# Memory attention and a maxout FFN on one core: who issues the first loads, how many transfers k and the last outputs take

## The chip, the cores and the metric

The kernel runs on one core of a Trainium2 chip. Its engines are TensorE (PE; PEld is its weight load), VectorE (DVE), ScalarE (ACT), GpSimd (POOL) and SyncE (SP); SP, ScalarE and GpSimd issue DMA transfers, which 16 DMA engines carry out. The metric is the time of one execution on the device in microseconds, the median of several runs.

## The reference

Eight batches of eight heads, 576 positions, 64 values a head and 32 memory slots; then a feed-forward layer over the 4608 rows of 512. All inputs and the output are float32.

```python
# q, k, v: (8, 8, 576, 64); phi: (8, 8, 576, 32); w1, w2, w3: (512, 768); w_out: (768, 512)
a = softmax(phi, axis=2)                        # over the 576 positions
k_m = einsum('bhsm,bhsd->bhmd', a, k)
v_m = einsum('bhsm,bhsd->bhmd', a, v)
attn = softmax(q @ k_m.T / 8, axis=-1)          # over the 32 slots
x = (attn @ v_m) as rows of (batch, position), columns of (head, value)
h = maximum(maximum(x @ w1, x @ w2), x @ w3)
out = h @ w_out
```

## The kernel before

The program has no loop over batches at run time. All steps are Python functions, and a long string of tokens, written out by hand, gives the order in which they emit their instructions: `B0@1` is part 0 of step `B` for batch 1, and a `!` swaps the engine that does the step's side work. Each engine runs its own instructions in that order and waits on semaphores for the others. Two strings of this kind matter here: the tokens (lines 782 to 809) and the PSUM banks (lines 143 to 151), which are handed out in order of request.

**Loads.** Tokens `L`, `H` and `J` load phi, k, v and q of a batch, `Y` the weights. k, v, q and the weights are cast to bfloat16 on the way and are issued by GpSimd (lines 97, 112, 119, 126), as is phi for all batches but the first (line 93). For batch 0, `load_ph` has SP issue two transfers, one for each half of the head pairs (line 91), and k comes as two transfers too: tokens `H2@0`, then `H0@0`, both through `load_kv` (line 97). The first instruction of ScalarE is the load of its table of functions (line 62). Each transfer of GpSimd takes the next of eight semaphores and waits until the transfer eight before it has landed; SP and ScalarE share another eight, taken in turn in the order of the program. SP, ScalarE's sends and the last outputs all count there. At the end (traced as the last line of the launch code, L837) SP waits for the last transfer on each of these semaphores in their order.

**Attention of a batch.** `E` is exp of phi (ScalarE, line 234), `B` multiplies it with k, v and a column of ones (TensorE, line 256), `N` and `K` norm and transpose the result, `Q` transposes q, `S` makes the scores and their exp (lines 342, 351). For batch 0 TensorE runs products of a zero tile (`Z`, line 164) while it waits.

**The feed-forward layer.** `D` folds v_m into the weights (line 453). w3 is subtracted from w1 and w2, so that the maximum can be taken in fewer steps; `V` does these subtractions in pieces (`w_diff`, line 218) and is emitted for pieces 0, 2 and 1. `F` multiplies the weights with the attention (line 504) and takes the maximum (line 517). The product with w_out is done by `T` (`ffn2`, lines 667 to 685) for batches 0 and 1 and for the rows between two batches, and by `P` (`products`, line 615) for the others: seven products that VectorE and ScalarE combine into four quarters of an output tile `ot`. `products` has SP send a tile of 512 KB when its second half is done (line 652); for the last batch each half is sent alone, 256 KB.

**The end.** `T4@7` calls `ffn2_last`: the last 128 rows are made in two halves of 256 columns. VectorE copies the left half from PSUM and SP sends it (lines 737, 738); ScalarE copies and sends the right half (lines 740, 741). The tile that both write is the buffer of an output tile of batch 6, since `opool` has four buffers.

Of the kernel before, what the change touches and what calls it, by code (L numbers as in the profile page):

```python
# [15 lines left out]
def kernel(  # L16
# [12 lines left out]
    nc = tc.nc  # L29
# [29 lines left out]

    nc.scalar.preload_act_table_set("natural_log_exp_and_others")
    KV, KS = NP * NC * D, D + 1
    K1 = NP * NC * KS
    ones_k = [const.tile([P, D + KV], BF16, name=f"ko{i}") for i in range(2)]
# [19 lines left out]
    def load_ph(b):  # L85
        ph = inp.tile([P, NP, NC, M], FP32, name="ph", tag="ph")
        loaded.setdefault(b, {})["ph"] = ph
        dst = ph.rearrange("p j c m -> p j (c m)")
        if b == 0:
            for h in halves:  # L90
                nc.sync.dma_start(out=dst[:, h], in_=by_pair(phi, b)[:, h])
        else:
            nc.gpsimd.dma_start(out=dst, in_=by_pair(phi, b))

# [31 lines left out]
        nc.gpsimd.dma_start(out=wo_sb, in_=moe_w_out.rearrange("(t p) c -> p t c", p=P))  # L126

    load_ph(0)

    warm = const.tile([P, BANK], BF16, name="warm")  # L130
    nc.vector.memset(warm, 0.0)  # L131
# [21 lines left out]
    def one_bank():  # L153
        return psum[:, int(next(banks))]
# [57 lines left out]

    def w_diff(n, swap):

        c, end = n * BANK, (n + 1) * BANK
        while c < end:
            e = min(end, (c // DF + 1) * DF)
            (nc.gpsimd if swap else nc.vector).tensor_tensor(  # L218
                out=w12[:, :, c:e],
                in0=w12[:, :, c:e],  # L220
                in1=w_sb[:, :, 2, c % DF : c % DF + e - c],
                op=ALU.subtract,
            )
            c = e
# [356 lines left out]
    def products(b, i, swap):  # L581

        s, a = sums(b), blocks(b)
        wp3 = wp3s[b]

        def plain(r, c):
            return lambda k, q: a[r][c][:, k, q]

        def summed(n):
            src = a[1][0] if n == 2 else s[min(n, 2)]  # L590
            return lambda k, q: src[:, k, q]

        def w_plain(i, j):
            c = slice(CH * j, CH * (j + 1))
            return lambda k: wo_sb[:, KT * i + k, c] if k < KT else wp3[:, i, c]

        def w_summed(n):
            return lambda k: tw[:, n, k] if k < KT else twb[b % 2][:, n]

        lhs, rhs, name = [  # L600
            (summed(0), w_summed(0), "y"),
            (plain(0, 0), w_plain(0, 0), "x"),
            (plain(0, 1), w_plain(1, 0), "z"),
            (summed(3), w_plain(1, 1), "y"),
            (summed(1), w_summed(1), "x"),
            (summed(2), w_summed(2), "x"),
            (plain(1, 1), w_summed(3), "x"),
        ][i]
        acc = quads.setdefault(b, {})
        if i < 3:  # L610
            acc[name] = one_bank()
        po = acc[name]
        for k in range(KT + 1):
            for q in range(2):
                nc.tensor.matmul(  # L615
                    po[:, q * CH : (q + 1) * CH],
                    lhsT=lhs(k, q),
                    rhs=rhs(k),
                    start=(i < 3 and k == 0 and q == 0),
                    stop=(k == KT and q == 1),  # L620
                    skip_group_check=True,
                )
        x = po.rearrange("p (q n) -> p q n", q=2)

        def copy(out_, in_):
            if swap:
                nc.vector.tensor_copy(out=out_, in_=in_)
            else:
                nc.scalar.copy(out=out_, in_=in_)  # L629

        if i in SNAP:
            t = ln if i == 0 else work.tile([P, S], FP32, name="snap", tag="r")
            t = acc[SNAP[i]] = t[:, 0:DM].rearrange("p (q n) -> p q n", q=2)
            copy(t, x)
        acc[i] = True
        done = [2] if i == 2 else [i] if i > 4 else [4] if 3 in acc and 4 in acc else []
        for n in done:
            if ("ot", n // 5) not in acc:
                acc["ot", n // 5] = opool.tile([P, 2, DM], FP32, name="ot")
            ot = acc["ot", n // 5][:, :, slice(0, CH) if n in (2, 6) else slice(CH, DM)]  # L640
            if n == 6:
                copy(ot, x)
            else:
                if n == 4:
                    x = acc["y"].rearrange("p (q n) -> p q n", q=2)
                y = acc[{2: "m1", 4: "u2", 5: "m5"}[n]]
                nc.vector.tensor_tensor(out=ot, in0=x, in1=y, op=ADD)
            if n in (4, 6) or b == B - 1:
                r0 = b * S + (b % 2) * HP
                rows = out[r0 : r0 + 2 * TW].rearrange("(q r p) c -> p q r c", q=2, r=2)  # L650
                c = slice(0, DM) if b < B - 1 else slice(0, CH) if n in (2, 6) else slice(CH, DM)
                nc.sync.dma_start(
                    out=rows[:, :, n // 5, c], in_=acc["ot", n // 5][:, :, c]
                )

    osts = {}

    def ffn2(b, t, swap):

# [2 lines left out]
        c0 = S - HP if t == 4 else (b % 2) * (S + HP) + t * P  # L662
        if b == B - 1:
            return ffn2_last(b, c0)
        po = one_bank()
        for n, fc in enumerate(fts[b]):
            nc.tensor.matmul(  # L667
                po,
                lhsT=hT[:, row(fc), c0 : c0 + P],
                rhs=wo_sb[:, fc, :],  # L670
                start=(n == 0),
                stop=False,
            )
        for g in range(NG):
# [31 lines left out]
    def ffn2_last(b, c0):  # L706
# [18 lines left out]
        for i, (c, po) in enumerate(zip(cs, pos)):  # L725
# [9 lines left out]
            rows = out[r0 : r0 + P, c]  # L735
            if i == 0:
                nc.vector.tensor_copy(out=ot[:, c], in_=po)
                nc.sync.dma_start(out=rows, in_=ot[:, c])
            else:
                nc.scalar.copy(out=ot[:, c], in_=po)  # L740
                nc.scalar.dma_start(out=rows, in_=ot[:, c])

    def issue(b, n, swap):
# [29 lines left out]
            "W": lambda: w3_t(i, swap),  # L773
            "g": lambda: send(i),
            "d": lambda: fold_begin(i),
            "O": lambda: w3_o(i, swap),
            "V": lambda: w_diff(i, swap),
            "Z": lambda: warm_up(i),
# [1 line left out]


    for w in """
        E@0 H2@0 H0@0 L3@0 Z25@0 B0@0 Y2@0 I@0 N0@0 Z2@0 K0@0! Q0@0 Q1@0 Z9@0 S@0 Z2@0
        M0@0 M1@0 R0@0 R1@0 W0@0 Y3@0 W1@0 W2@0 Z6@0 O1@0 H3@0 O3@0 O2@0 H1@0 X1@0 B1@0
        X0@0 N1@0 K1@0 O0@0 Y0@0 D1@0! D0@0! D3@0 F8@0 Y1@0 F10@0! L0@1 L1@1 F6@0 J0@1
        F0@0! F2@0! D2@0 D4@0 F4@0 F1@0 F3@0 F5@0 F11@0 F7@0 V0@0! E@1 F9@0 B0@1 N0@1
        T2@0! J1@1 Q0@1 L2@1 Q1@1 V2@0 K0@1! T1@0 S@1 B1@1 V1@0 L3@2 N1@1 M1@1 a0@1 s0@1
        R1@1 c0@1 K1@1 T3@0 D2@1 m0@1! D0@1 X1@1 L1@2 X0@1 D1@1 Q0@2 L0@2 T0@0! L2@2
        L1@3 Q1@2 L0@3 r0@2 F8@1! F4@1 F6@1! F7@1 E@2 F10@1! F2@1 F5@1 F0@1 g2@0 B@2
        D3@1 L2@3 L3@3 N@2 F9@1 F3@1 K@2! F11@1 g1@0 S@2 F1@1 D1@2! E@3 L1@4 U2@9 D0@2  # L790
        D3@2 T3@1 U0@9 T4@1! L0@4 r0@3 a@2 s@2 c@2 D2@2 B@3 L2@4 m@2! U2@2 X@2 F10@2 N@3
        F2@2 F11@2 F4@2 F0@2 K@3! L3@4 Q0@3 Q1@3 F6@2 F1@2 F8@2 g0@0 F3@2 S@3 F7@2 a@3
        F5@2 g3@0 s@3 F9@2 r0@4! E@4 U0@2 c@3 L0@5 U1@9 m@3! T2@1 X@3 U3@9 D0@3 D3@3
        T0@1! T1@1 L1@5 D2@3 B@4 D1@3! N@4 P1@2! L2@5 Q1@4 U1@2 F2@3 F6@3 F3@3 F8@3 L3@5
        U3@2 L1@6 U0@3 A0@2! Q0@4 K@4! F4@3! F0@3 F9@3 P2@2! A1@2! S@4 A2@2! A3@2! F5@3
        E@5 a@4 P4@2 F1@3 r0@5 P0@2 L2@6 F10@3 L0@6 s@4 F7@3 c@4 P5@2 m@4 D1@4! D3@4
        U1@3 F11@3 P3@2 A0@3! D2@4 B@5 A2@3! N@5 D0@4 X@4 T4@3! L1@7 A1@3! F10@4 Q0@5
        K@5 F0@4 L3@6 Q1@5 P6@2! S@5 r0@6! F11@4 F2@4! F1@4 L0@7 F6@4 F4@4! P1@3 F8@4
        a@5 s@5 U2@3 D2@5 D3@5 c@5 P2@3! E@6 m@5 A3@3! F5@4 P4@3 F3@4 F9@4 P0@3 D1@5!
        X@5 B@6 N@6 L2@7 D0@5 P5@3 U3@3 F8@5! F7@4 P3@3! r0@7! L3@7 U0@4 F2@5! F10@5 E@7  # L800
        U0@5 F3@5 Q0@6 A0@4! U1@4 P6@3 F11@5 F4@5 Q1@6 F6@5 F9@5 K@6! F0@5 A2@4! U2@4
        F5@5 S@6 F7@5 A1@4! a@6 A3@4! B@7 N@7 s@6 D3@6 D1@6! P0@4 P1@4 U3@4 K@7! P2@4!
        F1@5 Q1@7 P4@4 c@6 D0@7 D1@7 D0@6 P3@4 P5@4 U0@6 Q0@7 m@6 X@6 D2@6 D3@7 D2@7!
        A0@5! T4@5 S@7 A1@5! P6@4 F0@6 a@7 s@7 F4@6 F10@6 F1@6 c@7 F2@6 U2@5 F6@6 P1@5
        F3@6 F7@6 U1@5 P2@5 F8@6 A3@5! F9@6 F11@6 P4@5 m@7 X@7 F5@6 P0@5! F6@7 F10@7!
        A2@5! F2@7 P3@5! F4@7! F0@7 P5@5 F8@7! F1@7 F11@7 A0@6! U3@5 P6@5 F5@7 F9@7 U0@7
        A1@6 U1@7 A2@6 F3@7 U1@6 P1@6 F7@7 P0@6 P2@6! P4@6 U2@6 P1@7 A0@7 A3@6 U3@6 A1@7
        U3@7! P2@7! P5@6! P3@6 U2@7! A2@7 A3@7 P4@7 P6@6 P0@7! P5@7 P3@7! P6@7 T4@7!
    """.split():
        n, b = w.rstrip("!").split("@")  # L810
        issue(int(b), n, w.endswith("!"))
# [30 lines left out]
```

## Time and profile before

| | us |
|---|---|
| median of three runs | 162.17 (161.5, 162.17, 162.24) |
| profiled execution | 162.39 |
| its span | 160.6 (1.77 us of the execution lie outside it) |
| TensorE busy | 149.8 |
| VectorE, ScalarE, GpSimd busy | 118.5, 98.2, 104.3 |
| GpSimd's queue, SP's queue, ScalarE's queue: share of the 16 DMA engines' span | 70.9%, 15.3%, 2.2% |
| HBM read, written | 39.32 MB, 9.44 MB |

The granted TensorE clock is full throughout (1.0). In the page, the span is cut into 40 slices of 4 us; a digit is the busy share in tenths. In a timeline a line holds the start, the duration, the engine, the line of the kernel, the operation and, in brackets, the idle time ahead of it with what ended it. A "q" behind an engine's name (SPq) marks its issuing of transfers. In the windows a row holds the stretch and its length, the busy time of PE, PEld, DVE, ACT and POOL, the granted clock, the DMA engines' share and GB/s. The packet and landing records are the trace's lists of the DMA engines' packets and of the 16 completions of each transfer, one an engine.

### The profile page before, as it was taken

The page shows a single profiled execution, that of the slowest core. Times are in us where ns is not written, and L with a number is a line of the kernel's source. Part 1 is how long each engine was busy: PE and PEld are TensorE (multiplying, and loading weights), DVE is VectorE, ACT ScalarE, POOL GpSimd, SP SyncE. Part 2 cuts the span into 40 slices and gives each one's busy share as a digit, 9 for nine tenths or more (in the row PEclk, how much of TensorE's full clock was granted, in tenths as well). Part 3 has the DMA queues.
Part 4 walks back from the last instruction along what each step waited for, and adds up shares of the span by engine and source line. Part 5 has one row for each costly group of instructions (what it writes and reads, how often), then busy time and mean ns, then how long its engine had stood idle before and what let it go on. Part 6 is the DMA issues. An engine that isn't in the chain of part 4 may idle for free.

```text
span 160.6 us, 5165 instructions
## 1 busy us (share of the span) xinstructions
PE 149.8 (93%) x2219; PEld 100.4 (62%) x2228; DVE 118.5 (74%) x205; ACT 98.2 (61%) x140; POOL 104.3 (65%) x98
## 2 busy tenths in 40 slices
PE   7978698979897999999999999999999999999991
PEld 2433444654455537636877577787774888888871
DVE  2023803699897897897998789898989869799851
ACT  3205435742786699997777789888876944224210
POOL 7932101993039949968999996999969996910000
PEclk9999999999999999999999999999999999999999
DMA  5999999999999999999999999999803500330374
GB/s 150 164 201 203 201 209 214 279 207 212 209 276 245 276 233 261 285 262 282 268 231 209 259 260 254 261 173 170 271 0 134 196 6 0 131 131 4 150 279 159
DMA packets 22342, 31.78 MB, mean 198 GB/s; under 512 B 1072, under 2 KB 17456, under 8 KB 22320
## 3 DMA queue, kind: packets, MB, share of 16 engines
q0 software_dynamic: 16096, 21.43, 70.9%
q1 hardware_dynamic: 5504, 8.85, 15.3%
q10 hardware_dynamic: 720, 1.18, 2.2%
q8 instruction: 17, 0.28, 0.7%
q14 instruction: 5, 0.04, 0.1%
HBM read 39.32 MB, written 9.44 MB: 304 GB/s over the span
## 4 chain that ended last, share of the span: by engine, by line
PE 63%; DMA 25%; POOL 6%; issue 2%; ACT 1%; DVE 1%; POOLq 0%
PE psum L504 23%; PE psum L615 23%; DMA w_sb<-in_moe_w_dram 14%; DMA kvr<-in_v_dram 10%; PE psum L667 6%; PE psum L453 4%; PE psum L256 3%; PE psum L342 2%; POOL qq L112 1%; DMA out_dram<-ot 1%; POOL kvr L97 1%; POOL ko L97 1%; PE psum L676 1%; PE psum L685 1%; POOL w_sb L119 1%
## 5 line engine op out<-in xcount | busy, mean ns | idle before, releaser
L504 PE MATMUL psum<-hx,wp 128*128 128x288 bf16 x384 | 53.2, 286 | 0.1
L504 PEld LDWEIGHTS <-wp 128*128 128x128 bf16 x384 | 36.3, 98 | 11.6 <-issue 2.1
L517 DVE TENSOR_TENSOR hx<-psum,h 128x576 bf16<-128x576 f32 x48 | 34.8, 749 | 6.3 <-PE psum L504 4.5
L177 ACT CAST wp<-psum 128x1024 bf16<-128x1024 f32 (+1 forms) x29 | 27.5, 993 | 4.6 <-PE psum L453 4.4
L175 ACT ACTIVATE h<-psum 128x576 bf16<-128x576 f32 x34 | 21.5, 655 | 7.2 <-PE psum L504 6.6
L615 PEld LDWEIGHTS <-hx 128*128 128x128 bf16 x192 | 18.4, 98 | 3.5 <-issue 1.1
L667 PE MATMUL psum<-wo_sb,hx 128*128 128x512 bf16 x60 | 15.6, 380 | 0.3
L351 ACT ACTIVATE e<-psum 128x576 bf16<-128x576 f32 x16 | 9.5, 649 | 6.2 <-PE psum L342 6.2
L164 PE MATMUL psum<-warm 128*128 128x512 bf16 x42 | 12.0, 440 | 1.4 <-DVE warm L131 1.2
L615 PEld LDWEIGHTS <-w_sb 128*128 128x128 bf16 x120 | 11.6, 98 | 2.4 <-issue 0.8
L321 DVE STREAM_TRANSPOSE qT<-qq 128x576 f32<-128x576 f32 x16 | 11.9, 760 | 1.1 <-DMA qq<-in_q_dram 1.0
L107 POOL COPY kvr<-ko 128x2304 bf16<-128x2304 bf16 x3 | 6.3, 2111 | 8.8 <-DMA ko<-in_k_dram 8.8
L629 ACT COPY snap<-psum 128x512 f32<-128x512 f32 x11 | 6.5, 594 | 8.7 <-PE psum L615 8.7
L540 POOL TENSOR_TENSOR w_sb<-hx 128x1024 bf16<-128x1024 bf16 x5 | 10.6, 2121 | 1.6 <-DVE hx L517 1.6
L234 ACT ACTIVATE e<-ph 128x1152 bf16<-128x1152 f32 (+1 forms) x9 | 9.6, 1067 | 2.4 <-DMA ph<-in_phi_dram 2.4
L218 POOL TENSOR_TENSOR w_sb<-w_sb 128x2048 bf16<-128x2048 bf16 x1 | 4.1, 4052 | 10.6 <-PE psum L453 10.6
L179 DVE TENSOR_SCALAR h<-psum 128x576 bf16<-128x576 f32 x14 | 10.3, 746 | 0.7 <-PE psum L504 0.6
L667 PEld LDWEIGHTS <-hx 128*128 128x128 bf16 x66 | 5.9, 98 | 7.5 <-issue 1.7
L256 PEld LDWEIGHTS <-e 64*32 64x32 bf16 x720 | 7.3, 89 | 5.1 <-issue 3.6
L427 POOL TENSOR_TENSOR t<-t,sm 128x1152 bf16<-128x1152 bf16 x4 | 8.5, 2124 | 3.0 <-DVE sm L420 1.7
L540 POOL TENSOR_TENSOR twb<-wp 128x256 bf16<-128x256 bf16 x11 | 7.4, 675 | 4.2 <-ACT wp L177 4.2
L177 ACT COPY ot<-psum 128x512 f32<-128x512 f32 x9 | 5.3, 595 | 7.7 <-PE psum L676 6.8
(102 smaller groups left out, 280.6 us busy)
## 6 DMA issues: line engine op xcount, KB each, us to landing
out_dram<-ot SPq DMA_DIRECT2D x10, 512.0 KB, 3.3
qq<-in_q_dram POOLq DMA_DIRECT2D x7, 576.0 KB, 11.0
ph<-in_phi_dram POOLq DMA_DIRECT2D x7, 576.0 KB, 14.6
ko<-in_k_dram POOLq DMA_DIRECT2D x7, 576.0 KB, 16.6
kvr<-in_v_dram POOLq DMA_DIRECT2D x7, 576.0 KB, 11.1
out_dram<-ot SPq DMA_DIRECT2D x11, 256.0 KB, 6.1
w_sb<-in_moe_w_dram POOLq DMA_DIRECT2D x3, 768.0 KB, 19.0
out_dram<-ot ACTq DMA_DIRECT2D x4, 256.0 KB, 6.8
```

Source lines behind the costliest of these rows:

```text
L164: nc.tensor.matmul(po[:, 0:BANK], lhsT=warm[:, 0:P], rhs=warm, start=True, stop=True)
L175: nc.scalar.activation(out=out_, in_=in_, func=AF.Relu)
L177: nc.scalar.copy(out=out_, in_=in_)
L179: nc.vector.tensor_scalar_max(out=out_, in0=in_, scalar1=0.0)
L234: nc.scalar.activation(out=s["e"][:, js], in_=loaded[b]["ph"][:, js], func=AF.Exp)
L256: nc.tensor.matmul(kvp[M * j : M * (j + 1), a, 0:nd], lhsT=s["e"][r, j, c, :], rhs={None: lambda: k_and_v(b, r, j, c), 0: lambda: ones_and ...
L321: nc.vector.transpose(out=s["qT"][:, j].rearrange("p j c r e -> p (j c r e)").bitcast(FP32), in_=loaded[b]["q"][:, j].rearrange("p j c d - ...
L504: nc.tensor.matmul(acc[:, h, 0:SH], lhsT=wps[b][:, g, w * DF + ft * P : w * DF + (ft + 1) * P], rhs=attn[:, g, c0 : c0 + SH], start=(g == ...
L517: nc.vector.tensor_tensor(out=hT[:, row(ft), (b % 2) * S : (b % 2 + 1) * S].rearrange("p (h n) -> p h n", h=2), in0=a, in1=s["h1", ft], op ...
L540: eng.tensor_tensor(out=out_, in0=in0, in1=in1, op=op)
L615: nc.tensor.matmul(po[:, q * CH : (q + 1) * CH], lhsT=lhs(k, q), rhs=rhs(k), start=(i < 3 and k == 0 and q == 0), stop=(k == KT and q == 1 ...
L667: nc.tensor.matmul(po, lhsT=hT[:, row(fc), c0 : c0 + P], rhs=wo_sb[:, fc, :], start=(n == 0), stop=False,)
```

## The change

Six places, all in how work is issued:

- `load_ph`: of batch 0's phi, the first half is issued by SP and the second by ScalarE; the load of ScalarE's table comes behind it in the program.
- The tokens `H2@0 H0@0` become `L1@0`: batch 0's k is one transfer of GpSimd.
- `w_diff` has four pieces instead of three, and the tokens `V1@0 V3@0` stand where `V1@0` stood.
- `ffn2_begin` (token `t`) does the first four matmuls of `ffn2`; each `t` stands right ahead of its `T`.
- `products` sends each half of batch 6's output tiles alone, as it does for batch 7.
- `ffn2_last`: SP sends the left half as two transfers of 64 rows.

```diff
-    nc.scalar.preload_act_table_set("natural_log_exp_and_others")
...
         if b == 0:
-            for h in halves:
-                nc.sync.dma_start(out=dst[:, h], in_=by_pair(phi, b)[:, h])
+            for eng, h in zip((nc.sync, nc.scalar), halves):
+                eng.dma_start(out=dst[:, h], in_=by_pair(phi, b)[:, h])
...
     load_ph(0)
+    nc.scalar.preload_act_table_set("natural_log_exp_and_others")
...
     def w_diff(n, swap):
-        c, end = n * BANK, (n + 1) * BANK
+        c, end = [(0, BANK), (BANK, DF), (2 * BANK, 2 * DF), (DF, 2 * BANK)][n]
...
-            if n in (4, 6) or b == B - 1:
+            if n in (4, 6) or b >= B - 2:
...
-                c = slice(0, DM) if b < B - 1 else slice(0, CH) if n in (2, 6) else slice(CH, DM)
+                c = slice(0, DM) if b < B - 2 else slice(0, CH) if n in (2, 6) else slice(CH, DM)
...
+    def ffn2_begin(b, t):
+        po = opened[b, t] = one_bank()
+        hT, c0 = hts[b // 2], (b % 2) * (S + HP) + t * P
+        for n, fc in enumerate(fts[b][0:4]):
+            nc.tensor.matmul(po, lhsT=hT[:, row(fc), c0 : c0 + P], rhs=wo_sb[:, fc, :],
+                             start=(n == 0), stop=False)
...
-        po = one_bank()
-        for n, fc in enumerate(fts[b]):
+        early = (b, t) in opened
+        po = opened[b, t] if early else one_bank()
+        for n, fc in enumerate(fts[b][4 if early else 0 :]):
...
-                nc.sync.dma_start(out=rows, in_=ot[:, c])
+                for r in (slice(0, HP), slice(HP, P)):
+                    nc.sync.dma_start(out=rows[r], in_=ot[r, c])
...
-        E@0 H2@0 H0@0 L3@0 Z25@0 B0@0 ...
+        E@0 L1@0 L3@0 Z25@0 B0@0 ...
...
-        T2@0! ... T1@0 S@1 B1@1 V1@0 L3@2 ... T3@0
+        t2@0 T2@0! ... t1@0 T1@0 S@1 B1@1 V1@0 V3@0 L3@2 ... t3@0 T3@0
```

More of the change, by code (lines that the diff above doesn't have):

```diff
@@ L654, in products @@
                 )
-    osts = {}
+    osts, opened = {}, {}
+    def ffn2_begin(b, t):
+        po = opened[b, t] = one_bank()
+        hT, c0 = hts[b // 2], (b % 2) * (S + HP) + t * P
+        for n, fc in enumerate(fts[b][0:4]):
+            nc.tensor.matmul(
+                po,
+                lhsT=hT[:, row(fc), c0 : c0 + P],
+                rhs=wo_sb[:, fc, :],
+                start=(n == 0),
+                stop=False,
+            )
     def ffn2(b, t, swap):
@@ L670, in ffn2 @@
                 rhs=wo_sb[:, fc, :],
-                start=(n == 0),
+                start=(n == 0 and not early),
                 stop=False,
@@ L775, in issue @@
             "d": lambda: fold_begin(i),
+            "t": lambda: ffn2_begin(b, i),
             "O": lambda: w3_o(i, swap),
@@ L782 @@
     for w in """
[L783 to L806, printed above, removed]
@@ L807 @@
-        A1@6 U1@7 A2@6 F3@7 U1@6 P1@6 F7@7 P0@6 P2@6! P4@6 U2@6 P1@7 A0@7 A3@6 U3@6 A1@7
-        U3@7! P2@7! P5@6! P3@6 U2@7! A2@7 A3@7 P4@7 P6@6 P0@7! P5@7 P3@7! P6@7 T4@7!
+        E@0 L1@0 L3@0 Z25@0 B0@0 Y2@0 I@0 N0@0 Z2@0 K0@0! Q0@0 Q1@0 Z9@0 S@0 Z2@0 M0@0
+        M1@0 R0@0 R1@0 W0@0 Y3@0 W1@0 W2@0 Z6@0 O1@0 H3@0 O3@0 O2@0 H1@0 X1@0 B1@0 X0@0
+        N1@0 K1@0 O0@0 Y0@0 D1@0! D0@0! D3@0 F8@0 Y1@0 F10@0! L0@1 L1@1 F6@0 J0@1 F0@0!
+        F2@0! D2@0 D4@0 F4@0 F1@0 F3@0 F5@0 F11@0 F7@0 V0@0! E@1 F9@0 B0@1 N0@1 t2@0
@@ new lines @@
+        T2@0! J1@1 Q0@1 L2@1 Q1@1 V2@0 K0@1! t1@0 T1@0 S@1 B1@1 V1@0 V3@0 L3@2 N1@1 M1@1
+        a0@1 s0@1 R1@1 c0@1 K1@1 t3@0 T3@0 D2@1 m0@1! D0@1 X1@1 L1@2 X0@1 D1@1 Q0@2 L0@2
+        t0@0 T0@0! L2@2 L1@3 Q1@2 L0@3 r0@2 F8@1! F4@1 F6@1! F7@1 E@2 F10@1! F2@1 F5@1
+        F0@1 g2@0 B@2 D3@1 L2@3 L3@3 N@2 F9@1 F3@1 K@2! F11@1 g1@0 S@2 F1@1 D1@2! E@3
+        L1@4 U2@9 D0@2 D3@2 t3@1 T3@1 U0@9 T4@1! L0@4 r0@3 a@2 s@2 c@2 D2@2 B@3 L2@4
+        m@2! U2@2 X@2 F10@2 N@3 F2@2 F11@2 F4@2 F0@2 K@3! L3@4 Q0@3 Q1@3 F6@2 F1@2 F8@2
@@ new lines @@
+        g0@0 F3@2 S@3 F7@2 a@3 F5@2 g3@0 s@3 F9@2 r0@4! E@4 U0@2 c@3 L0@5 U1@9 m@3! t2@1
+        T2@1 X@3 U3@9 D0@3 D3@3 t0@1 T0@1! t1@1 T1@1 L1@5 D2@3 B@4 D1@3! N@4 P1@2! L2@5
+        Q1@4 U1@2 F2@3 F6@3 F3@3 F8@3 L3@5 U3@2 L1@6 U0@3 A0@2! Q0@4 K@4! F4@3! F0@3
+        F9@3 P2@2! A1@2! S@4 A2@2! A3@2! F5@3 E@5 a@4 P4@2 F1@3 r0@5 P0@2 L2@6 F10@3
+        L0@6 s@4 F7@3 c@4 P5@2 m@4 D1@4! D3@4 U1@3 F11@3 P3@2 A0@3! D2@4 B@5 A2@3! N@5
+        D0@4 X@4 T4@3! L1@7 A1@3! F10@4 Q0@5 K@5 F0@4 L3@6 Q1@5 P6@2! S@5 r0@6! F11@4
@@ new lines @@
+        F2@4! F1@4 L0@7 F6@4 F4@4! P1@3 F8@4 a@5 s@5 U2@3 D2@5 D3@5 c@5 P2@3! E@6 m@5
+        A3@3! F5@4 P4@3 F3@4 F9@4 P0@3 D1@5! X@5 B@6 N@6 L2@7 D0@5 P5@3 U3@3 F8@5! F7@4
+        P3@3! r0@7! L3@7 U0@4 F2@5! F10@5 E@7 U0@5 F3@5 Q0@6 A0@4! U1@4 P6@3 F11@5 F4@5
+        Q1@6 F6@5 F9@5 K@6! F0@5 A2@4! U2@4 F5@5 S@6 F7@5 A1@4! a@6 A3@4! B@7 N@7 s@6
+        D3@6 D1@6! P0@4 P1@4 U3@4 K@7! P2@4! F1@5 Q1@7 P4@4 c@6 D0@7 D1@7 D0@6 P3@4 P5@4
+        U0@6 Q0@7 m@6 X@6 D2@6 D3@7 D2@7! A0@5! T4@5 S@7 A1@5! P6@4 F0@6 a@7 s@7 F4@6
@@ L809 @@
+        F10@6 F1@6 c@7 F2@6 U2@5 F6@6 P1@5 F3@6 F7@6 U1@5 P2@5 F8@6 A3@5! F9@6 F11@6
+        P4@5 m@7 X@7 F5@6 P0@5! F6@7 F10@7! A2@5! F2@7 P3@5! F4@7! F0@7 P5@5 F8@7! F1@7
+        F11@7 A0@6! U3@5 P6@5 F5@7 F9@7 U0@7 A1@6 U1@7 A2@6 F3@7 U1@6 P1@6 F7@7 P0@6
+        P2@6! P4@6 U2@6 P1@7 A0@7 A3@6 U3@6 A1@7 U3@7! P2@7! P5@6! P3@6 U2@7! A2@7 A3@7
+        P4@7 P6@6 P0@7! P5@7 P3@7! P6@7 T4@7!
     """.split():
```

## The prediction

> **What bounds the kernel now.** I read the page first, then the windows of the span, the chain that ended last, and the timelines of both ends.
>
> ```profile
> span 160.6 us, 5165 instructions
> PE 149.8 (93%) x2219; PEld 100.4 (62%) x2228; DVE 118.5 (74%) x205; ACT 98.2 (61%) x140; POOL 104.3 (65%) x98
> DMA  5999999999999999999999999999803500330374
> ```
>
> PE is busy almost throughout, and the DMA engines from the second slice (4 us each) to the 29th. The chain tells which of the two sets the time where:
>
> ```profile
> 8.08 22.20 DMA w_sb<-in_moe_w_dram
> ...
> 35.01 16.53 DMA kvr<-in_v_dram
> 51.68 0.80 PE psum L256 x72
> ...
> 143.94 10.56 PE psum L615 x96
> ```
>
> Up to 51.68 us the chain is two long transfers, queued behind what GpSimd issued earlier; from there it is nearly all TensorE. So there are three stages: a DMA stream to 51.7, TensorE to 157.4, and a tail to 160.6. In the windows TensorE is busy 104.75 of the 105.4 us from 52 to 157.4: what the stream gains or loses by 51.68 is passed on one for one. The limit for a gain is TensorE's wait ahead of that line, 0.97 us.
>
> In the first stage the question is whether the stream can start sooner, or runs dry:
>
> ```profile
> 1.00:2.00 1.00, 0.81 (x2) 0.28 (x3) 0.72 (x11) 1.00 (x1) 0.75 (x1) 1.00 0.19 24
> 2.00:3.00 1.00, 1.00 (x4) 0.43 (x3) 0.00 (x0) 0.02 (x1) 1.00 (x3) 1.00 0.92 256
> 3.00:4.00 1.00, 1.00 (x4) 0.33 (x3) 0.00 (x0) 0.24 (x1) 1.00 (x2) 1.00 1.04 323
> 9.00:10.00 1.00, 0.70 (x72) 0.69 (x72) 0.00 (x0) 0.00 (x0) 0.56 (x1) 1.00 1.19 202
> ```
>
> The last two columns are the DMA share and GB/s. The share is at 0.92 in the third microsecond and stays over 1 to the end of the stage (1.13 to 1.23 from 14 to 52): the engines are full before anything of k has moved. In the packet records the first phi packet starts at 1.83, the first of GpSimd's queue at 3.7, and phi's last at 4.3.
>
> ```profile
> 0.74 1.28 ACT L62 ACT_TABLE_LOAD   x1 [0.74 <-PEq L826]
> 0.74 0.93 SPq L91 DMA_DIRECT2D ph<-in_phi_dram  x2
> 1.25 1.60 POOL L97 DMA_DIRECT2D ko<-in_k_dram  x2 [0.80 <-POOLq L826]
> 4.63 0.68 ACT L234 ACTIVATE e<-ph 128x576 bf16<-128x576 f32 x1 [0.18 <-DMA ph<-in_phi_dram]
> 9.29 0.80 PE L256 MATMUL psum<-ko,e 64*32 64x128 bf16 x72 [0.41 <-DMA ko<-in_k_dram]
> ```
>
> Two phi issues follow each other on SP, two k issues on GpSimd; exp of phi is done at 5.31, and TensorE begins at 9.29, when k has landed. The tail, in the timeline and in the instructions of the last line:
>
> ```profile
> 157.22 0.34 SPq L738 DMA_DIRECT2D out_dram<-ot  x1
> 157.43 0.37 ACT L740 COPY ot<-psum 128x256 f32<-128x256 f32 x1 [1.39 <-DMA out_dram<-ot]
> 157.83 0.34 ACTq L741 DMA_DIRECT2D out_dram<-ot  x1
> L837 SPq EVENT_SEMAPHORE  x11: 17/28/28, 157.6 to 160.6; - x11
> ```
>
> ScalarE's last copy starts 0.04 us after the last matmul (157.39); the transfer named as its releaser is another's. Its own transfer, issued at 157.86, lands at 159.56. SP waits for the output semaphores in a fixed order of eight; this transfer holds the fifth, seen at 159.58, and the sixth, seventh and eighth follow at 159.64, 159.70 and 159.76.
>
> **The change, part by part**, against this execution (162.39 us: the span and 1.77 outside it; it is 0.22 above the median 162.17).
>
> *phi.* Both halves are issued at 0.74, one by SP and one by ScalarE, instead of 0.77 and 1.24 on SP. The table load moves behind one issue (0.34 on ScalarE, 0.42 to 0.46 on SP): it ends near 2.45 instead of 2.02, before the first half lands (3.77). What that hides behind: exp ends at 5.31 and k lands at 9.2, so even 3 us more would cost nothing. The gain can only be idle DMA time ahead of k. From 2.0 to 2.5 the engines are 83% busy, so 0.5 x 0.17 = 0.09 us; nothing is lost before that, since they are full from the first packet. Bounds: nothing, and the 0.46 us by which the second issue moves. I take 0.09, since the rows show full engines. The Trainium skill (Trainium Kernel Development and Optimization, Key Constraints) says that transfers issued from SP, ScalarE and GpSimd share the same DMA engines, so that several issuers only save issue time. The full share in the windows agrees; with all the issue time counted the term would be the 0.46.
>
> *k.* One issue less on GpSimd: q, w3 and all behind it are issued about 0.8 earlier. That gains nothing by itself, as the queue never runs dry: in the packet records the engines go from k to q without a pause. GpSimd's semaphores rotate by eight; dropping the first transfer leaves every later wait on the same transfer as before, except w2's, which is gone and had not stalled (w1 and w2 are issued in one piece of 1.54). The next phi still waits for all of k (9.44 now). In the stream, 16 completion packets of 22 ns vanish, one an engine: 0.02 us. Where the descriptors of a whole transfer take longer to write, the stream starts later. The first half's issue took 0.89 and the second 0.72; whole transfers of twice the size take 0.77 (q) and 0.76 (w3), so the size adds about 0.05. The row nearest to that, q, speaks for no change in the first packet at 3.7. Bounds: -0.4 to +0.7 (a second 0.72 in full); I take -0.02. k's own landing has room: kvt is ready at 11.71, but the scores start at 13.18, behind q's landing at 12.0.
>
> The Trainium skill (DMA: Bandwidth & Descriptors, Anatomy of one DMA) gives each GpSimd transfer about 2.0 us fixed, mostly the write's completion. Taken as paid in a row, one transfer less would be worth 2 us, and the sum would end near 160. The trace speaks against it: the last landings of the two halves are 7.7 and 9.2, so 1.5 us apart, about what 295 KB take at the 190 GB/s of these windows.
>
> *The recut w_diff and ffn2_begin.* Each new step stands directly ahead of its partner in the order, and the issue order of both kernels on TensorE and VectorE has the same instructions in the same places. Zero.
>
> *Batch 6's outputs.* Four transfers of 256 KB instead of two of 512: two more issues of 0.37 on SP, which is idle between transfers. The first leaves SP near 146.5, where the DMA share is 0.04. The buffer of the last output is one of these; both its transfers land several microseconds before 156.8. Zero; without the cover it would be 0.37 each.
>
> *The last output.* The left half goes as two transfers of 64 rows on SP, the second issued about 0.4 after 157.22. Landing took 1.75 after the issue for the whole half, so it lands at about 159.35, 0.2 ahead of ScalarE's. The three added transfers move ScalarE's transfer from the fifth output semaphore to the eighth: nothing is left to check when it lands. That takes away 3 x 0.06 = 0.18 us. ScalarE's copy gets two more semaphores to wait for, checked while it is idle (1.39 us).
>
> Sum: 0.09 + 0.02 + 0.18 = 0.29 us. 162.39 - 0.29 = 162.10 for such an execution, 161.88 from the median.
>
> **Rivals.**
> 1. *The late engines catch up (faster).* In the landing records of k's first half, 12 of 16 engines are done by 6.1, three at 6.8 to 6.9, one at 7.7; for q and w3 the span from first to last is still 1.7. So a lag is born in the first GpSimd transfer and kept, and it is the last engine that TensorE waits for. If one transfer halves that lag, the stream gains 0.85: 161.88 - 0.85 = 161.0. The 0.97 us wait allows that. For: afterwards the late engines keep pace. Against: the same bytes, and the cause of the lag isn't shown. The skill's DMA page (Latency and other measured facts) says two of the engines are usually slower, perhaps because the descriptor rings share their ports. The trace agrees that two are last for q. Chance 0.18.
> 2. *The first k packet comes later (slower).* All descriptors of a transfer might have to be written before its first packet moves. At an added 0.72 the stream ends 0.7 later, less the 0.29: 162.17 + 0.43 = 162.6. From 0.27 it eats the gain; from 1.1 it is slower by 0.5%. Were the whole 2.45 us from the first issue to the first packet doubled: 164.3. Against: issues of 256 and 512 descriptors take nearly the same time. Chance 0.22, of it 0.1 for over 0.5%.
> 3. *Only the tail moves, or the split eats it.* If the phi term is nothing: 161.99. If SP's second piece or a shared issue path delays ScalarE's last transfer by 0.2 or more: 162.2. Chance 0.2.
>
> The forecast itself has 0.4.
>
> **How the numbers follow.** 0.5% of 162.17 is 0.81 us, about what a measurement of this kernel can tell from no change. Forecast and rival 3 lie within it, as does half of rival 2. Rival 1 with its end at 161.0 lies mostly outside. Faster 0.2, same 0.69, slower 0.11. The three times of before lie from 161.5 to 162.24, which adds 0.3 to either side. The range goes from 161.0 (rival 1) to 162.8 (rival 2 at 0.72 with that scatter).
>
> **What would show it.** ScalarE's table load at about 1.15; one k issue at 1.25 and GpSimd's first packet at 3.7; TensorE's first L256 between 9.0 and 9.4; the L256 of batch 2 at 51.4 to 51.7 (51.68 now); the last matmul 0.1 earlier than 157.39; the last landing 1.7 us after ScalarE's issue and no semaphore waits behind it. If the batch 2 line moves by more than 0.3 either way, the k or phi term is wrong; if the span after the last landing does not shrink by 0.18, the tail term is.

## The result, and the profile after

| | before | changed |
|---|---|---|
| median of nine runs | 161.54 us (161.13 to 162.24) | 162.88 us (162.2 to 163.13) |
| profiled execution, its span | 162.39, 160.6 | 162.84, 161.1 |

The ratio is 1.0068, with a 95% interval of 1.0049 to 1.0087: the change makes the kernel slower by 0.8 to 1.4 us. The forecast was no change: 161.9 us, in a range from 161.0 to 162.8. With nine runs it shows that before's profiled execution lay 0.85 us above its median, and the changed kernel's at its own. So the two profiles differ by less (0.45) than the kernels do, and a stage of before may not be read from one execution to a few tenths.

The page of the changed kernel:

```profile
span 161.1 us, 5171 instructions
PE 150.7 (94%) x2219; PEld 100.5 (62%) x2228; DVE 118.2 (73%) x205; ACT 97.9 (61%) x140; POOL 103.6 (64%) x97
DMA  5999999999999999999999999999803500332554
```

The instruction counts of TensorE, VectorE and ScalarE are those of before; GpSimd has one less. The shape of the span is the same: DMA to the 29th slice, TensorE to the end. The chain that ended last:

```profile
7.35 23.56 DMA w_sb<-in_moe_w_dram
...
35.84 15.89 DMA kvr<-in_v_dram
51.87 0.80 PE psum L256 x72
```

The weights are issued 0.7 us sooner than before, yet their wait is 1.4 us longer (23.56 instead of 22.20). What GpSimd issues behind them comes 0.83 later (35.84 instead of 35.01), and batch 2's first product 0.19 later than in before's profiled execution. The head of the timeline shows where this begins:

```profile
0.74 0.45 SPq L90 DMA_DIRECT2D ph<-in_phi_dram  x1
0.74 0.48 ACTq L90 DMA_DIRECT2D ph<-in_phi_dram  x1
1.25 0.93 POOL L96 DMA_DIRECT2D ko<-in_k_dram  x1 [0.80 <-POOLq L843]
1.26 1.28 ACT L128 ACT_TABLE_LOAD   x1 [1.26 <-PEq L843]
4.13 1.26 ACT L234 ACTIVATE e<-ph 128x576 bf16<-128x576 f32 x2 [1.59 <-DMA ph<-in_phi_dram]
10.09 0.80 PE L256 MATMUL psum<-ko,e 64*32 64x128 bf16 x72 [1.38 <-DMA ko<-in_k_dram]
```

phi and the table load do what was foreseen: exp is done at 5.39. But k, one transfer now, lands at 9.95 instead of 9.16, and TensorE waits 1.38 us for it. One stretch of the windows from the kernel before, then two from the changed one (the last three columns are the granted clock, the DMA share and GB/s):

```profile
7.00:8.00 1.00, 1.00 (x6) 0.48 (x5) 0.00 (x0) 0.00 (x0) 1.00 (x2) 1.00 1.19 182
...
7.00:8.00 1.00, 1.00 (x6) 0.49 (x5) 0.00 (x0) 0.00 (x0) 1.00 (x2) 1.00 1.07 131
12.00:14.00 2.00, 2.00 (x7) 0.64 (x5) 1.01 (x2) 0.37 (x1) 0.74 (x1) 0.50 1.16 210
```

From 7 to 8 us the DMA engines moved 131 GB/s, where before moved 182. And TensorE, which had waited just ahead, is granted half its clock from 12.0 to 15.4.

The tail, in the timeline and in the instructions of SP's last sends:

```profile
157.41 1.16 SPq L753 DMA_DIRECT2D out_dram<-ot  x2
157.61 0.37 ACT L755 COPY ot<-psum 128x256 f32<-128x256 f32 x1 [1.39 <-PE psum L741]
158.02 0.37 ACTq L756 DMA_DIRECT2D out_dram<-ot  x1
L753 SPq DMA_DIRECT2D out_dram<-ot x2: 533/556/578, 157.4 to 158.0; - x2
```

A transfer of 64 rows takes SP 533 to 578 ns to issue; the one of 128 rows took 345. The second starts at 158.00, level with ScalarE's (158.02), and lands at 160.08, when ScalarE's (159.80) is already there. From the start of ScalarE's last copy to the end of the span it is 3.45 us, before 3.19.

### The profile page after: what moved, and what is told of

The parts are those of the page before. It is cut to its first block, busy times and chain, and to the rows that moved or that the text cites. A ratio compares the mean times of both kernels' runs of the same rounds, so it can differ in the third digit from the quotient of the medians.

```text
span 161.1 us, 5171 instructions
## 1 busy us (share of the span) xinstructions
PE 150.7 (94%) x2219; PEld 100.5 (62%) x2228; DVE 118.2 (73%) x205; ACT 97.9 (61%) x140; POOL 103.6 (64%) x97
## 4 chain that ended last, share of the span: by engine, by line
PE 64%; DMA 24%; POOL 6%; issue 2%; ACT 1%; DVE 0%; POOLq 0%
PE psum L615 23%; PE psum L504 23%; DMA w_sb<-in_moe_w_dram 15%; DMA kvr<-in_v_dram 10%; PE psum L453 4%; PE psum L681 4%; PE psum L256 3%; PE psum L663 2%; PE psum L342 2%; POOL qq L111 1%; POOL kvr L96 1%; PE psum L690 1%; PE psum L699 1%; POOL ko L96 1%; POOL w_sb L118 1%
## 5 line engine op out<-in xcount | busy, mean ns | idle before, releaser
L615 PEld LDWEIGHTS <-hx 128*128 128x128 bf16 x192 | 18.4, 98 | 3.5 <-issue 1.1
L164 PE MATMUL psum<-warm 128*128 128x512 bf16 x42 | 13.5, 484 | 1.4 <-DVE warm L131 1.2
L218 POOL TENSOR_TENSOR w_sb<-w_sb 128x2048 bf16<-128x2048 bf16 x1 | 4.1, 4067 | 10.4 <-PE psum L453 10.4
L276 DVE RECIPROCAL rden<-psum 128x2 f32<-128x2 f32 x8 | 1.3, 164 | 12.2 <-PE psum L256 12.1
L164 PEld LDWEIGHTS <-warm 128*128 128x128 bf16 x44 | 4.9, 118 | 8.0 <-issue 4.6
L615 PE MATMUL psum<-wo_sb,hx 128*128 128x256 bf16 x72 | 9.8, 273 | 0.0
```

Of the source, the lines that this page charges most:

```text
L164: nc.tensor.matmul(po[:, 0:BANK], lhsT=warm[:, 0:P], rhs=warm, start=True, stop=True)
L615: nc.tensor.matmul(po[:, q * CH : (q + 1) * CH], lhsT=lhs(k, q), rhs=rhs(k), start=(i < 3 and k == 0 and q == 0), stop=(k == KT and q == 1 ...
```

## The experiments

Each ratio is against before in runs on the same chip; times in us are what the ratio makes of before's median. Behind a ratio stands its 95% interval.

**Each part alone.** First k:

```diff
-        E@0 H2@0 H0@0 L3@0 Z25@0
+        E@0 L1@0 L3@0 Z25@0
```

> The kernel before with batch 0's k as one transfer, nothing else changed. Theory A (one transfer of k lands later and delays the stream): k lands near 10.0 us instead of 9.2, q near 13.0 instead of 12.0, and the time rises by 0.4 to 1.0 us. Theory B (the loss is made in the tail, by the split of the last output): no change within 0.2 us, k may land late but the DMA stream absorbs it before batch 2. Rival C (ScalarE's issue of phi and the later table load cost it): no change.

Ratio 1.0058 (1.0028 to 1.0087), 0.9 us slower: nearly the whole loss. The execution that was profiled was the fastest of its twelve (161.18 us, the median 162.56); there k landed at 8.71 and batch 2 began at 50.47. So k in one transfer isn't late each time, and this profile shows the lucky case.

Then phi, with ScalarE's issue ahead of the table load:

```diff
-            for h in halves:
-                nc.sync.dma_start(out=dst[:, h], ...)
+            for eng, h in zip((nc.sync, nc.scalar), halves):
+                eng.dma_start(out=dst[:, h], ...)
```

> The kernel before with only the second half of the first phi issued by ScalarE ahead of its table load. Theory A: no change (within 0.2 us), k lands at 9.1 to 9.2. Theory B: no change. Rival C: 0.4 us or more slower, with the first product of TensorE after 9.6.

1.0007 (0.9982 to 1.0033): nothing to be seen, k at 9.08, the first product at 9.22. Rival C falls.

The split of the last output:

```diff
-                nc.sync.dma_start(out=rows, in_=ot[:, c])
+                for r in (slice(0, HP), slice(HP, P)):
+                    nc.sync.dma_start(out=rows[r], in_=ot[r, c])
```

> The kernel before with only the left half of the last output sent as two transfers of 64 rows. ScalarE's last transfer takes the sixth output semaphore. Theory B: SP's second piece is issued only about 0.6 us after the first and lands behind ScalarE's transfer; from the last matmul to the end of the span 3.5 us instead of 3.2, so 0.3 us slower. Theory A alone: 0.06 us faster (one semaphore check less). Rival C: the same 0.06.

1.0018 (0.9996 to 1.0041). The profile has the same issues as the changed kernel,

```profile
L739 SPq DMA_DIRECT2D out_dram<-ot x2: 533/556/580, 156.8 to 157.4; - x2
```

the last landing 0.28 us behind ScalarE's, and 3.56 us from ScalarE's last copy (0.04 behind the last matmul) to the end of the span instead of 3.19. The time's interval just includes no change; the trace shows 0.37. SP's second piece, which lands last, holds the fifth semaphore, as ScalarE's transfer did before, so no check is saved here.

Batch 6's sends in halves (`b == B - 1` becomes `b >= B - 2`, and `b < B - 1` becomes `b < B - 2`):

> The kernel before with only batch 6's output tiles sent in halves; ScalarE's last transfer takes the seventh semaphore. All theories: 0.12 us faster from two semaphore checks less, 3.1 us from the last matmul to the end of the span; if the earlier sends also empty the DMA queues ahead of the last transfer, up to 0.3 us faster. If the rotation of the semaphores costs a wait, slower.

0.9988 (0.9963 to 1.0012). In the trace 3.09 us from ScalarE's last copy to the end, 0.10 less than before: the two checks that are saved, and no more.

**Parts undone.** The two runs of this part also leave out the recut `w_diff` and `ffn2_begin`. That takes nothing away: in the traces TensorE, VectorE and ScalarE execute the same sequence of 2219, 205 and 140 instructions before, in the changed kernel and in e6. First the changed kernel with the last output in one transfer again:

> The changed kernel without the split of the last output (k, phi and batch 6's sends as changed; ScalarE's last transfer takes the seventh semaphore). If the parts add up: k +0.94, phi 0, batch 6 -0.1, so 0.8 us slower than before, with 3.08 us from the last matmul to the end of the span instead of 3.44 in the changed kernel. If the split costs nothing in the whole change: as slow as the changed kernel, 1.1 us.

1.0042 (1.0017 to 1.0067), 0.7 us, near the sum; the interval, 0.3 to 1.1 us, does not separate it from the changed kernel's loss. And the changed kernel with k in two again (`L1@0` back to `H2@0 H0@0`):

> The changed kernel with batch 0's k in two transfers again; phi's issue, batch 6's sends and the split of the last output stay. If the one transfer of k is the main loss: 0.2 to 0.3 us slower than before (the tail's 0.26), k's landing at 9.0 to 9.6 and clock 1.0. If the loss sits in what remains: 0.7 us or more slower.

0.9994 (0.9971 to 1.0017): undoing this one edit takes the loss away. The split's cost stays in its trace (3.44 us from ScalarE's last copy to the end), but is not seen in the times.

**By which way does late k reach the end?** Six more products of the zero tile (`Z25@0` becomes `Z31@0`) let TensorE start late, with the DMA stream as before:

> The kernel before with 31 instead of 25 products of the zero tile ahead of batch 0, nothing else: TensorE reaches its first product with k about 0.85 us later (10.1 to 10.2 us), while k and the whole DMA stream are as before. It separates two ways from k's late landing to the end. Theory P (TensorE's late start passes down the chain of batch 0): 0.6 to 0.9 us slower. Theory S (the late DMA engines delay every later transfer, and TensorE's start has room): within 0.2 us of before.

0.9981 (0.9960 to 1.0002): TensorE's late start costs nothing. The span of its profile is 252.8 us at a clock of 0.564, so no line is read from it, and how late TensorE was in the timed runs isn't shown. The other profiles say the same: in the changed kernel TensorE begins to transpose w3 1.97 us later than before (17.71 against 15.74), 0.96 behind w3's landing, yet its next products start 0.04 us behind the landing of w_out in both (20.57 and 19.74). So it is the stream that passes the delay on.

**Why is one transfer slow?** Merged into one, k also brings forward all that GpSimd issues behind it. Here the identity and the ones columns are made right behind k's issue:

```diff
-        E@0 H2@0 H0@0 L3@0 Z25@0 B0@0 Y2@0 I@0 N0@0
+        E@0 L1@0 I@0 L3@0 Z25@0 B0@0 Y2@0 N0@0
```

> The kernel before with k as one transfer, and GpSimd's work on the identity and the ones columns moved from behind w3's issue to right behind k's, so that q, w3 and what follows are issued as late as before or later. Theory A1 (the transfers queued behind k come too early and slow k's own end): the loss goes, within 0.3 us of before. Theory A2 (the size of the first transfer alone makes it end late): 0.9 us slower, as with k in one transfer.

1.0047 (1.0025 to 1.0069): q's issue was back at 2.90, and k landed (10.55) later than in any other profile that is read:

```profile
10.69 0.80 PE L256 MATMUL psum<-ko,e 64*32 64x128 bf16 x72 [1.90 <-DMA ko<-in_k_dram]
```

Theory A1 falls. Next, k in two unequal transfers (`load_kv` for pair 0, then for pairs 1 to 3):

> The kernel before with k in two transfers of unequal size, one head pair (147 KB) first and three pairs (442 KB) behind it. Theory A2 (what counts is when the first transfer of GpSimd's queue completes, since the engines stall there once): as before or up to 0.3 us faster. Theory A1 (the second issue of GpSimd keeps q away from k's end): as before. If a large transfer is slow wherever it stands: between, 0.4 to 0.9 us slower.

0.9996 (0.9974 to 1.0018): as before. A transfer of 442 KB behind one of 147 KB costs no time that can be seen. Then a later pair merged, batch 0's v (`H3@0` and `H1@0` become `L2@0`):

> The kernel before with batch 0's v in one transfer instead of two, k in two as before. Theory F (only the first transfer of GpSimd's queue makes engines late): within 0.2 us of before, the last engine 1.0 to 1.3 us behind the median for q and for v. Theory G (any larger transfer costs): 0.5 us or more slower.

1.0003 (0.9980 to 1.0026): nothing to be seen; in its profile the last engine is 1.5 us behind the median for q and 1.3 for v. And the next transfer, q, cut in two behind the whole k (`L1@0 J0@0 J1@0`):

> The kernel before with k as one transfer and q, right behind it, as two. Theory F without repair: 0.8 to 1.0 us slower, as with k in one, the last engine still about 2 us behind at w3. If the borders between small transfers let late engines catch up: the lag at w3 is near 1.2 us and the loss under 0.4 us.

1.0047 (1.0020 to 1.0074): no repair. So the cut counts in k, at the head of GpSimd's queue, and not in v or q behind it. That the first transfer's own size decides is not shown: k in 147 and 442 KB (e9) and k in four of 147 KB (below, 0.9970) begin with the same transfer, and their intervals overlap.

The landing records show what goes with it. This is how far, for q, the last of the 16 DMA engines was behind the median one, in each profiled execution:

| k | lag for q, us |
|---|---|
| one transfer | 1.9 (changed), 2.1, 2.0; 1.2 and 1.2 in the two executions that were the fastest of their kernels (e1, e16) |
| two | 1.0 (before), 1.1, 0.8, 1.1, 1.2, 1.2, 1.5; 2.1 in e9, an execution that was the slowest of its kernel |
| four (below) | 0.7, 0.4, 0.9 |

A few engines, two to five, are late from k on. In the changed kernel the lag is 1.9 for every transfer from q to 36 us. It is not always made by the first transfer: in e9's profile it is 0.65 for that and 2.55 for the second, and with k in two it grew on the way in other executions too (before: 1.0 for q, 2.1 for batch 1's k at 35.6).

TensorE waits for the last engine, and GpSimd, by way of TensorE, does so too. Before and changed:

```profile
27.32 4.05 POOL L218 TENSOR_TENSOR w_sb<-w_sb 128x2048 bf16<-128x2048 bf16 x1 [10.65 <-PE psum L453]
31.32 0.74 POOL L112 DMA_DIRECT2D qq<-in_q_dram  x1
...
28.15 4.07 POOL L218 TENSOR_TENSOR w_sb<-w_sb 128x2048 bf16<-128x2048 bf16 x1 [10.41 <-PE psum L453]
32.15 0.74 POOL L111 DMA_DIRECT2D qq<-in_q_dram  x1
```

TensorE's first product of step `D` (L453) starts within 0.1 us of w1's landing (26.31 before, 27.16 changed), and about 1.0 later GpSimd starts the first piece of `w_diff` (L218, 4.05 us). Only when that ends does GpSimd issue the next transfers: 5.0 to 5.1 us after w1's landing in all sixteen profiles that are read. (The chain puts this stretch down to the weight that lands last, at 30.3 and 30.9; the subtraction was still running then.) Where the issue comes at 31.6 or earlier (eleven profiles), the median DMA engine needs 1.4 us from the landing of the transfer ahead to that of this q; where it comes at 32.15 or later (five), 1.7 to 2.6. By the difference, 0.2 to 1.2 us, the queue ran dry there for the median engine. Of these five, three have k in one (changed, e5, e7), and two have k in two (e8, e9, each the slowest execution of its kernel). Their lag at w1 is 1.9 to 2.6, in the others 0.7 to 1.4. It is not the whole account: from this issue to batch 2's first product it is 18.7 to 20.4 us, since lags made later count as well. In before's profile the lag is 2.5 at batch 2's v, in the changed kernel's 1.9.

That k is late in many runs, and not in the profiled ones alone, is seen from TensorE's clock, which each run reports: among the runs that the ratios use it was under 0.992 in 17 of 56 of the five kernels with k in one transfer (half clock for 3.4 us, as above, makes 0.989), and in 1 of 116 of the others (before and e14 left out).

What is shown is that k in one transfer makes the loss (e1 adds it, e6 takes it away), and by which instructions a late landing delays the stream. That the lag is what a single k makes worse fits the profiles, but no run set the lag alone, and why some engines are late, and why later with k in one, stays open.

**Better versions.** Three early transfers more (batch 6's halves and one tile of batch 5 in halves), no split at the end:

```diff
-            if n in (4, 6) or b == B - 1:
+            alone = b >= B - 2 or (b == B - 3 and n < 5)
+            if n in (4, 6) or alone:
...
```

> The kernel before with batch 6's output tiles and one tile of batch 5 sent in halves, k and phi and the last output as before: three transfers more, all early, put ScalarE's last transfer on the eighth semaphore. By the tail theory 0.18 us faster than before, 3.0 us from the last matmul to the end of the span. If the added sends cost SP or the DMA engines something: no gain.

0.9986 (0.9966 to 1.0006): not clear of no change. In the trace it is 0.91 us from the last landing to the end of the span instead of 1.09: the 0.18 of three checks. From ScalarE's last copy it is 3.07, only 0.12 less than before, since the last transfer took 0.06 longer to land. Then k in four:

```diff
-        E@0 H2@0 H0@0 L3@0
+        E@0 k0@0 k1@0 k2@0 k3@0 L3@0
...
+            "k": lambda: load_kv(b, 0, slice(i, i + 1)),
```

> The kernel before with batch 0's k in four transfers of one head pair each. If every further cut of the first transfers lets the late DMA engines catch up: k lands at 9.0 or before, last engine less than 1.5 us behind the median one, and the time is 0.2 to 0.5 us below before. If two transfers are enough and the third and fourth only add issues (q's issue moves from 2.85 to about 4.4): same within 0.2 us, or slower by up to 0.5 us if the queue runs dry.

0.9970 (0.9946 to 0.9993), 0.5 us faster, k at 8.20. Both together:

> k in four transfers together with the early halves of batches 5 and 6 that put ScalarE's last transfer on the eighth semaphore. If both parts hold and add up: the four transfers' effect less another 0.2 us, from the last matmul to the end of the span 3.0 us.

0.9953 (0.9934 to 0.9973), 0.8 us faster than before (median 161.12 against 161.81). Its timeline at both ends:

```profile
1.25 2.33 POOL L97 DMA_DIRECT2D ko<-in_k_dram  x4 [0.80 <-POOLq L828]
8.83 0.80 PE L256 MATMUL psum<-ko,e 64*32 64x128 bf16 x72
...
156.17 0.34 SPq L739 DMA_DIRECT2D out_dram<-ot  x1
156.37 0.37 ACT L741 COPY ot<-psum 128x256 f32<-128x256 f32 x1 [1.39 <-PE psum L728]
156.77 0.34 ACTq L742 DMA_DIRECT2D out_dram<-ot  x1
```

TensorE waits for k no more: the products of the zero tile end last. With q in two as well:

> k in four transfers, q in two, and the early halves of batches 5 and 6 (the kernel of e12_four_eighth with q cut). Theory F: as e12, 0.6 to 0.9 us faster than before, since the lag is settled by the first transfers. With repair at every border: another 0.2 us. If the two more issues of GpSimd let the queue run dry: 0.2 to 0.5 us worse than e12.

0.9972 (0.9953 to 0.9990): no better than e12.

## Why the prediction was wrong

**What held.** The stages, and the passing on one for one: from batch 2's first product to ScalarE's last copy it is 105.75 us before and in the changed kernel, and 105.73 in e1. The phi term is too small to be seen (a gain of 0.09 expected; e2 measured a loss of 0.1, with an interval from a gain of 0.3 to a loss of 0.5). The first packet of k came at 3.59, before 3.69, so rival 2 did not happen: the one issue took 0.93 instead of 0.89, as its 0.05 said. The recut steps left the instructions as they were. The checks that are saved are worth 0.06 each.

**The step that failed: the k term.** I took -0.02 between bounds of -0.4 and +0.7; e1 measured 0.9. I priced the start of the transfer (issue, first packet) and its bytes, but not its end, and the end is set by the last engine. The reason given, that the queue never runs dry since the engines go from k to q without a pause, is true of the sum over 16 engines there and says nothing of the few that are late, nor of 34 to 37 us, where a late issue lets the others run dry. Rival 1 had much of it: a lag that is there from k on, and that TensorE waits for. But it let the merge only halve it. The runs have the other sign: mostly about 1 us behind at q with k in two, about 2 in three of five profiles with one, 0.4 to 0.9 with four. The slack named for k itself (scores at 13.2) was there, as e14 shows; it doesn't help, since the later transfers are late by as much.

**The split.** It was zero, with SP's second piece 0.2 ahead of ScalarE's transfer; alone it is a loss of 0.37 (e3). The issue of 64 rows was set equal to that of 128 (0.34 to 0.4); it is 0.53 to 0.58 each. So in the changed kernel SP's second piece lands last, 0.28 behind ScalarE's, and it holds the seventh semaphore: two checks are saved, not three, and the tail is 0.26 longer instead of 0.18 shorter. The second half of rival 3, that the split eats the gain, came true and more.

**The base.** The forecast started from a median of three runs, 162.17; nine give 161.54. Of the miss of 1.0 us against 161.9 the changes account for 1.6 (a loss of 1.3 between the medians instead of a gain of 0.3), the base for 0.6 the other way. The profile read for the forecast lay higher still, and so the sign named for a wrong k term, batch 2's first product moved by more than 0.3, did not come: it moved by 0.19.

**The clock.** That a late k would halve TensorE's clock was not foreseen. The row is 0.50 from 12 to 14 us, behind a wait of 1.38. The Trainium skill (TensorE: Matmul & The Clock Gate, HAM oscillation) has the drop come with idle gaps over about 3.4 us; here it came behind waits of 1.38 and 1.90 (e7), so the measurement decides. It did not come behind waits of 1.58 (e8) and 1.67 (e5), so the length of the wait alone doesn't set it, and what does is open. It cost nothing: in the changed kernel and in e7 TensorE's products with w_out started 0.04 us behind its landing, as before.

## What to carry to other kernels

Don't merge the first load of a queue only because that saves issues: try the cut first, and read a landing from its last engine. Follow a late landing to the instruction that issues the next transfers; where it delays them, the engines that were on time run dry too. Price a transfer at the end of a kernel by the issue time of its own shape, and keep late additions off the path: semaphore positions can be shifted by early transfers just as well. Before pricing tenths from one profile, look where its time lies among the kernel's runs.

## What the runs showed of the hardware that was not expected

- Batch 0's k, the first load of GpSimd's queue: 590 KB at once is 0.8 to 0.9 us slower for the whole kernel than two transfers of 295 KB (e1, e7, e16), and four of 147 KB are 0.5 us faster. The Trainium skill (DMA: Bandwidth & Descriptors, Rules for kernel authors) advises one large transfer over many small ones; for v, later in the queue, merging made no difference (1.0003), and for k it is the wrong way round here.
- Issuing 64 rows of 1 KB from SP takes 533 to 580 ns, 128 rows 345.
- TensorE's clock was halved for 3.4 us after waits of 1.4 and 1.9 us, but not after waits of 1.6 and 1.7 in two other kernels.
